# A fused attention, expert and feed-forward kernel: float64 weights converted by one scaling and three bitwise instructions, in pieces twice as wide, with fewer of them in the last expert

## The chip, the cores and the metric

The kernel runs on one core of a Trainium2 chip. The metric is device time in microseconds (us) of one execution; the time before is 629.21, the median of three runs (628.65 to 629.40). The engines are named as in the profile: PE (matmuls; PEld its weight loads), DVE (VectorE), ACT (ScalarE), POOL (GpSimd) and SP (SyncE, which issues most transfers).

## What is computed

Three layers in a row on 1536 tokens of 512 columns: an attention with four sink keys and a window of 128, a mixture of eight experts that gives each token to one of them, and a feed-forward layer with 2048 hidden columns. The change touches the last:

```python
def _moe2_ref(x, w_in, w_out):
    h = x @ w_in
    r = np.maximum(h, 0.0)
    g = r * r
    return (g @ w_out).astype(np.float32)
```

w_in (512 x 2048) and w_out (2048 x 512) arrive as float64, since a float32 array divided or multiplied by a NumPy float64 scalar became float64. Each is 8 MB; the kernel reads them as pairs of 32-bit words and makes float32 values from them.

## The kernel before

**The order of the work.** The kernel is written by hand in the order in which each engine is to run it (a manual schedule), and every engine takes its instructions in that order. First comes the attention, then the eight experts, then the feed-forward layer. Matmuls are done in three products of high and low parts (`h` and `l`): a float32 matrix is rounded to a high part by a copy on ACT, and DVE subtracts that from the value to get the low part.

**Weights come through six buffers.** `raw_tile` gives one of NRAW = 6 buffers of 128 x 1024 words, half a megabyte each. A list `stream` holds all loads in their order: expert weights, then pieces of w_in and w_out. `pull` issues the next loads on SP while buffers are free; `freed` gives one back and, once `eager` is set, pulls at once. A transfer waits on SP until the last reader of its buffer is done, and whatever is behind it on SP waits too.

**A piece.** `piece_load` (L153) fetches one piece of a float64 matrix: for `("i", f)` the 128 hidden columns f of w_in, for `("o", f)` 128 rows of w_out; either is 128 x 512 float64. In the buffer the two words of a value lie side by side, `lo` and `hi`, so each is read and written with a stride of two words. `piece_stage` (L165) converts it in four stages:

- stage 0, on DVE: `lo` is shifted right by 29 and xored with a constant (L173); `hi`, shifted left by 3, is xored into it (L174), which gives the value's magnitude bits; and adding and subtracting 768 leaves the sign in `hi` (L175).
- stage 1, on ACT: the absolute value (L177) and the sign (L178).
- stage 2, on DVE: their product (L180).
- stage 3: the high part by a copy on ACT (L184) and the low part by a subtraction on DVE (L185), after which the buffer is free.

**Ticks.** `Ticks.tick` (L194) moves the conversion on by one: stage 3 of the piece three ticks back (LAG = 3), stage 0 of the next piece, stages 1 and 2 of the one before. The order of the pieces is i0, i1, i2, o0, o1, i3, o2, i4, o3 and so on (L928 to L932). Six ticks lie in the last expert's body, the others in the feed-forward layer, two in each step.

**An expert's body.** `body` (L835) handles one block of 128 tokens: first product in two halves (`g1`), ReLU on ACT (`relu`), transposes of the hidden values with their high and low parts (`tr`, which gives hTh on ACT at L868 and hTl on DVE at L869), second product (`g2`), and a scaling of the result by the gate (`ys`, L911, DVE), which POOL scatters. `plan` is a tuple of six numbers: how many items of `splits` are done in each of the six gaps between these parts. For experts 0 to 6 the items split the next expert's weights; for the last one they are ticks, by the tuple LAST, one in each gap. The body of the last expert also reads the first 512 tokens of the feed-forward layer back (`load_y`, transposes at L964, high and low part x2Ah and x2Al at L969 and L970), at points that the tuple ITS sets.

**The feed-forward layer.** It takes the tokens in four chunks of 512, 512, 256 and 256. A chunk has 16 steps, one per 128 hidden columns. In step f, `stage_a` makes the hidden columns with 12 matmuls (L1045), applies ReLU on ACT (L1047) and squares on DVE (L1048); `stage_g` makes the square's high part gh on ACT (L1056) and low part gl on DVE (L1057); `stage_b` multiplies the columns of the step before with w_out in 12 matmuls (L1069), of which the third is the first to read gl. PE thus takes a(f), b(f-1), a(f+1), b(f) and so on. In the first chunk one tick stands between `stage_a` and `stage_g`, another ahead of `stage_b`. Steps 7, 9, 11 and 13 also transpose 128 tokens each of the next chunk (x2T, x2Bh, x2Bl).

## Time and profile before

| what | value |
|---|---|
| median of three runs | 629.21 us (628.65 to 629.40) |
| the profiled execution | 631.66 us, its span 629.9 us |
| mean granted clock of PE in it | 0.99 of full speed |
| PE busy | 590.4 us, 94% of the span |
| PEld busy | 469.0 us, 74% |
| DVE busy | 377.4 us, 60% |
| ACT busy | 328.3 us, 52% |
| POOL busy | 135.8 us, 22% |
| last expert's body, first block | from about 288 us |
| feed-forward layer | 333.2 us to the end |

Times within the profile are us from the span's start. In rows of instructions in order of time, a number in brackets behind an instruction is how long its engine was idle before it, and behind the arrow what ended that. An engine that is idle costs nothing unless something on the way to the end waits for it.

### The profile page before, as it was taken

To read this page: it belongs to the slowest core of one execution; us is meant where nothing else is said; L and a number is where in the kernel's file an instruction comes from. 1 tells how busy PE (TensorE), PEld (TensorE's weight loads), DVE (VectorE), ACT (ScalarE), POOL (GpSimd) and SP (SyncE) were. 2 spreads that over 40 slices of the span, in tenths; PEclk is the share of its full clock that TensorE was granted. 3 is DMA by queue.
4 is the path that set the end of the run, shared out by engine and by line. 5 is a ranking of instruction groups with operands and counts; after the bars stand their busy time and mean duration, and the time that the engine had idled before them with its cause. 6 is when DMAs were issued, how large, how long until landed. Compare 5 with 4: busy or idle time off the path is not lost. (4 is left out here: it accounts for less than half of the span.)

```text
span 629.9 us, 9961 instructions
## 1 busy us (share of the span) xinstructions
PE 590.4 (94%) x3439; PEld 469.0 (74%) x3439; DVE 377.4 (60%) x943; ACT 328.3 (52%) x745; POOL 135.8 (22%) x235
## 2 busy tenths in 40 slices
PE   8999999969999999998898889889999999999994
PEld 4787777738887777776686667668888888999983
DVE  3788888646349967859826999995323223233321
ACT  4888887526248847656525767763222223233221
POOL 8444643351233323421101000000200001101001
PEclk9999999989999999999999999999999999999998
DMA  8696985345438956957654554530100000100000
GB/s 183 157 227 149 250 164 155 116 138 181 132 102 278 336 194 211 324 157 236 207 195 134 167 167 152 161 107 0 68 1 18 18 0 25 43 0 21 14 2 20
DMA packets 74795, 82.01 MB, mean 130 GB/s; under 512 B 42377, under 2 KB 53641, under 8 KB 74737
## 3 DMA queue, kind: packets, MB, share of 16 engines
q1 hardware_dynamic: 70736, 72.45, 40.1%
q0 software_dynamic: 4000, 8.82, 4.1%
q8 instruction: 32, 0.52, 0.3%
q14 instruction: 27, 0.21, 0.1%
HBM read 69.29 MB, written 16.27 MB: 136 GB/s over the span
## 5 line engine op out<-in xcount | busy, mean ns | idle before, releaser
L1048 DVE TENSOR_TENSOR xb<-xb 128x512 f32<-128x512 f32 (+1 forms) x64 | 35.7, 557 | 109.4 <-ACT xb L1047 109.4
L1047 ACT ACTIVATE xb<-a 128x512 f32<-128x512 f32 (+1 forms) x64 | 31.2, 488 | 116.5 <-PE a L1045 116.5
L1069 PE MATMUL out<-yh,gl 128*128 128x512 f32 x192 | 77.3, 403 | 10.7 <-DVE gl L1057 10.7
L1069 PE MATMUL out<-yh,gh 128*128 128x512 f32 x192 | 76.7, 399 | 0.1
L1069 PE MATMUL out<-yl,gh 128*128 128x512 f32 x192 | 75.9, 395 | 0.0
L1045 PE MATMUL a<-x2Ah,xh 128*128 128x256 f32 (+1 forms) x192 | 61.4, 320 | 0.3 <-PEq L1014 0.3
L1045 PE MATMUL a<-x2Al,xh 128*128 128x256 f32 (+1 forms) x192 | 61.3, 319 | 0.2 <-DVEq L1014 0.2
L1045 PE MATMUL a<-x2Ah,xl 128*128 128x256 f32 (+1 forms) x192 | 61.1, 318 | 0.0
L1077 POOL DMA_INDIRECT out_dram<-oo,tok x12 | 12.0, 998 | 221.9 <-DVE oo L1076 175.5
L447 ACT ACTIVATE p<-p,nm 128x260 f32<-128x260 f32 (+2 forms) x96 | 46.8, 489 | 17.1 <-DVE nm L435 15.9
L1069 PEld LDWEIGHTS out<-yh,gl 128*128 128x128 f32 x192 | 36.1, 188 | 24.7 <-DVE gl L1057 16.6
L1057 DVE TENSOR_TENSOR gl<-xb,gh 128x512 fp32r<-128x512 f32 (+1 forms) x64 | 35.7, 557 | 26.9 <-PE out L1069 14.4
L912 POOL DMA_INDIRECT yd<-ys,dst x14 | 25.3, 1809 | 120.7 <-POOLq L922 50.7
L1056 ACT CAST gh<-xb 128x512 fp32r<-128x512 f32 (+1 forms) x64 | 32.9, 514 | 34.0 <-DVE xb L1048 34.0
L140 DVE TENSOR_TENSOR yl<-raw,yh 128x512 fp32r<-128x512 f32 x64 | 40.4, 685 | 7.8 <-ACT yh L139 6.3
L1069 PEld LDWEIGHTS out<-yh,gh 128*128 128x128 f32 x192 | 36.1, 188 | 7.3 <-ACT gh L1056 1.0
L1069 PEld LDWEIGHTS out<-yl,gh 128*128 128x128 f32 x192 | 36.1, 188 | 7.1
L1045 PEld LDWEIGHTS a<-x2Ah,xh 128*128 128x128 f32 x192 | 36.1, 188 | 5.0 <-issue 0.7
L1045 PEld LDWEIGHTS a<-x2Al,xh 128*128 128x128 f32 x192 | 36.1, 188 | 4.7 <-DVEq L1014 0.5
L1045 PEld LDWEIGHTS a<-x2Ah,xl 128*128 128x128 f32 x192 | 36.4, 189 | 2.9
L139 ACT CAST xh<-raw 128x512 fp32r<-128x512 f32 x64 | 36.3, 619 | 1.0 <-DMA raw<-in_moe_w_dram 0.7
L869 DVE TENSOR_TENSOR hTl<-hT,hTh 128x512 fp32r<-128x512 f32 x28 | 19.3, 690 | 28.9 <-ACT hTh L868 25.7
(201 smaller groups left out, 1466.7 us busy)
## 6 DMA issues: line engine op xcount, KB each, us to landing
raw<-in_moe_w_dram SPq DMA_DIRECT2D x64, 512.0 KB, 5.0
raw<-in_moe_w_in_dram SPq DMA_DIRECT2D x16, 512.0 KB, 4.6
raw<-in_moe_w_out_dram SPq DMA_DIRECT2D x16, 512.0 KB, 3.4
yd<-zero SPq DMA_DIRECT2D x12, 256.5 KB, 5.7
xd<-x SPq DMA_DIRECT2D x12, 256.5 KB, 5.9
xb<-yd SPq DMA_DIRECT2D x12, 256.5 KB, 2.6
kr<-in_k_dram SPq DMA_DIRECT2D x12, 256.0 KB, 4.8
qr<-in_q_dram SPq DMA_DIRECT2D x12, 256.0 KB, 6.3
```

Of the source, the lines that this page charges most:

```text
L139: (hi or nc.scalar.copy)(self.h[i][:, sl], t[:, sl])
L140: (eng or nc.vector).tensor_sub(self.l[i][:, sl], t[:, sl], self.h[i].bitcast(F32)[:, sl])
L447: nc.scalar.activation(d["p"][:, h, :width], d["p"][:, h, :width], AF.Exp, bias=d["nm"][:, h : h + 1], scale=-1.0, accum_out=d["sm"][:, h ...
L869: nc.vector.tensor_sub(l_, p_, h_.bitcast(F32))
L912: nc.gpsimd.indirect_dma_start(out=yd[:, :], out_offset=bass.IndirectOffsetOnAxis(ap=dst[:, b, e : e + 1], axis=0), in_=y_, in_offset=None ...
L1045: nc.tensor.matmul(a_[:, :w], a, bb[:, kk, :w], start=(kk == 0 and m == 0), stop=(kk == KD - 1 and m == 2))
L1047: nc.scalar.activation(r_, a_[:, :w], AF.Relu)
L1048: nc.vector.tensor_mul(r_, r_, r_)
L1056: nc.scalar.copy(gh, r_)
L1057: nc.vector.tensor_sub(gl, r_, gh.bitcast(F32))
L1069: nc.tensor.matmul(outp[c][t], a[:, cs], bb[:, r], start=(f == 0 and m == 0), stop=(f == NFF - 1 and m == 2))
L1077: i = nc.gpsimd.indirect_dma_start(out=out, out_offset=bass.IndirectOffsetOnAxis(ap=tok[:, n : n + 1], axis=0), in_=o_, in_offset=None, bo ...
```

## The change

A piece is now 1024 columns of the destination: two neighbouring old pieces, a megabyte, in one double buffer. Three tiles of 128 x 2048 words take the place of the six buffers; expert weights use their halves as before, and so do the output tiles. A piece of w_in comes by two transfers, one of w_out by one.

The conversion has new instructions. ACT scales `hi`, read as a float32, by 2^-112, which moves the float64 exponent to the float32 one (L181 of the new kernel). DVE shifts `lo` right by 29 (L182), ors `hi` shifted left by 3 into it (L184), and ors the sign bit of `hi` into it (L185). Then follow the high part on ACT (L187) and the low part on DVE (L189). LAG is 1: a tick finishes the piece before and converts the next one up to its last bitwise instruction. There are 17 ticks rather than 35: three in the last expert's body, in its first, fourth and last gap, and one per step of the first chunk, between `stage_a` and `stage_g`; the one ahead of `stage_b` is gone.

```diff
-LAST = (1, 1, 1, 1, 1, 1)
+LAST = (1, 0, 0, 1, 0, 1)
...
+    RAW = [stage.tile([P, 2048], F32, name=f"raw{i}") for i in range(NRAW // 2)]
+
+    def raw_tile(n=1):
+
+        nonlocal slot
+        slot += slot % n
+        t = RAW[slot // 2 % len(RAW)][:, slot % 2 * 1024 : slot % 2 * 1024 + n * 1024]
+        slot += n
+        return t
...
-        while n and stream and held < NRAW:
-            held += 1
+        while n and stream and held + stream[0][0] <= NRAW:
+            held += stream[0][0]
             n -= 1
-            stream.pop(0)()
-
-    def freed():
+            stream.pop(0)[1]()
+
+    def freed(n=1):
...
+        t = raw_tile(2).bitcast(I32)
         if kind == "i":
+            w = 2 * P
+            for x in range(2):
+                nc.sync.dma_start(
+                    t[:, x * 1024 : x * 1024 + 1024].rearrange("p (k n) -> p k n", k=KD),
+                    w_in.rearrange("(k p) f -> p k f", p=P)[:, :, (2 * f + x) * w : (2 * f + x + 1) * w],
+                )
+        else:
             nc.sync.dma_start(
-                t.rearrange("p (k n) -> p k n", k=KD), w_in.rearrange("(k p) f -> p k f", p=P)[:, :, f * P * m : (f + 1) * P * m]
+                t.rearrange("p (t n) -> p t n", t=2), w_out[2 * f * P : 2 * (f + 1) * P, :].rearrange("(t p) n -> p t n", p=P)
             )
...
+        if n == 0:
+            nc.scalar.activation(hi.bitcast(F32), hi.bitcast(F32), AF.Copy, scale=2.0**-112)
+            nc.vector.tensor_scalar(lo, lo, 29, None, op0=ALU.logical_shift_right)
+        elif n == 1:
+            nc.vector.scalar_tensor_tensor(lo, in0=hi, scalar=3, in1=lo, op0=ALU.logical_shift_left, op1=ALU.bitwise_or)
+            nc.vector.scalar_tensor_tensor(lo, in0=hi, scalar=-(2**31), in1=lo, op0=ALU.bitwise_and, op1=ALU.bitwise_or)
+        elif n == 2:
+            nc.scalar.copy(w.h[f], lo.bitcast(F32))
         else:
-            val = t
-        if wide and n == 0:
-            nc.vector.tensor_scalar(lo, lo, 29, 0x40000000, op0=ALU.logical_shift_right, op1=ALU.bitwise_xor)
-            nc.vector.scalar_tensor_tensor(lo, in0=hi, scalar=3, in1=lo, op0=ALU.logical_shift_left, op1=ALU.bitwise_xor)
-            nc.vector.tensor_scalar(sg, sg, 768.0, -768.0, op0=ALU.add, op1=ALU.add)
-        elif wide and n == 1:
-            nc.scalar.activation(val, val, AF.Abs)
-            nc.scalar.activation(sg, sg, AF.Sign)
-        elif wide and n == 2:
-            nc.vector.tensor_mul(val, val, sg)
-        elif n == 3:
-            kind, f = p_
-            w, sl = WI if kind == "i" else WO, slice(f % 2 * 512, f % 2 * 512 + 512)
-            nc.scalar.copy(w.h[f // 2][:, sl], val)
-            nc.vector.tensor_sub(w.l[f // 2][:, sl], val, w.h[f // 2].bitcast(F32)[:, sl])
-            freed()
-
-    LAG = 3
+            nc.vector.tensor_sub(w.l[f], lo.bitcast(F32), w.h[f].bitcast(F32))
+            freed(2)
+
+    LAG = 1
...
-            for d, ns in ((LAG, (3,)), (0, (0,)), (1, (1, 2))):
+            for d, ns in ((LAG, (2,)), (0, (0,)), (LAG, (3,)), (0, (1,))):
...
-    NPRE = 3
-    order = [("i", f) for f in range(NPRE)] + [("o", 0), ("o", 1)]
-    for f in range(NPRE, NFF):
-        order += [("i", f), ("o", f - NPRE + 2)]
-    order += [("o", f) for f in range(NFF - NPRE + 2, NFF)]
+    NPRE = 2
+    order = [("i", f) for f in range(NPRE)]
+    for f in range(NPRE, NFF // 2):
+        order += [("o", f - NPRE), ("i", f)]
+    order += [("o", f) for f in range(NFF // 2 - NPRE, NFF // 2)]
...
-                o_ = stage.tile([P, DM], F32, tag="raw", name="oo", bufs=NRAW)
+                o_ = raw_tile()[:, :DM]
...
-        tick()
         if i >= 1:
             stage_b(*steps[i - 1])
```

On DVE, one step of the first chunk, before: from the square of a step (xb is its hidden columns) up to the first instruction of its second tick. raw is a buffer, x the weights w_in and y those of w_out, h and l their parts.

```order
L1048 TENSOR_TENSOR xb_196<-xb_196 128x512
L185 TENSOR_TENSOR xl_4994<-raw,xh_4993 128x512
L173 TENSOR_SCALAR raw<-raw 128x512
L174 SCALAR_TENSOR_TENSOR raw<-raw 128x512
L175 TENSOR_SCALAR raw<-raw 128x512
L180 TENSOR_TENSOR raw<-raw 128x512
L1057 TENSOR_TENSOR gl<-xb_196,gh 128x512
L185 TENSOR_TENSOR yl_5384<-raw,yh_5383 128x512
```

After the last row the five instructions of a piece follow once more, and then the next square. The same place after the change, with the next square:

```order
L1052 TENSOR_TENSOR xb_199<-xb_199 128x512
L182 TENSOR_SCALAR raw_75<-raw_75 128x1024
L189 TENSOR_TENSOR yl_5290<-raw_74,yh_5289 128x1024
L184 SCALAR_TENSOR_TENSOR raw_75<-raw_75 128x1024
L185 SCALAR_TENSOR_TENSOR raw_75<-raw_75 128x1024
L1061 TENSOR_TENSOR gl<-xb_199,gh 128x512
```

The whole conversion of a step stands between the square and gl; behind gl there is none.

On DVE, the first block of the last expert, before: from the first tick to the evictions of the first tokens.

```order
L173 TENSOR_SCALAR raw<-raw 128x512
L174 SCALAR_TENSOR_TENSOR raw<-raw 128x512
L175 TENSOR_SCALAR raw<-raw 128x512
...
L180 TENSOR_TENSOR raw<-raw 128x512
L869 TENSOR_TENSOR hTl<-hT,hTh 128x512
...
L970 TENSOR_TENSOR x2Al<-x2T,x2Ah 128x4x128
L185 TENSOR_TENSOR xl_4990<-raw,xh_4989 128x512
...
L970 TENSOR_TENSOR x2Al<-x2T,x2Ah 128x4x128 x3
```

And after the change, from the first tick to the gate's scaling:

```order
L182 TENSOR_SCALAR raw_76<-raw_76 128x1024
L184 SCALAR_TENSOR_TENSOR raw_76<-raw_76 128x1024
L185 SCALAR_TENSOR_TENSOR raw_76<-raw_76 128x1024
L873 TENSOR_TENSOR hTl<-hT,hTh 128x512
L182 TENSOR_SCALAR raw_74<-raw_74 128x1024
L189 TENSOR_TENSOR xl_4922<-raw_76,xh_4921 128x1024
...
L974 TENSOR_TENSOR x2Al<-x2T,x2Ah 128x4x128 x4
L182 TENSOR_SCALAR raw_75<-raw_75 128x1024
...
L915 TENSOR_SCALAR ys<-y,gate_2460 128x512
```

One tick, not two, stands ahead of the first hTl, and none between the evictions x2Al; the third stands behind them, ahead of ys.

## Rows read from the trace of the kernel before

**Rows 1.** Busy us by stretch: length, PE, PEld, DVE, ACT, POOL, clock, DMA share, GB/s.

```profile
333.20:436.70 103.50, 92.46 (x387) 70.30 (x388) 93.86 (x171) 69.92 (x119) 2.66 (x5) 1.00 0.43 135
436.70:527.70 91.00, 91.00 (x396) 73.32 (x395) 24.97 (x37) 21.56 (x36) 4.25 (x6) 1.00 0.05 18
```

**Rows 2.** Instructions in order of time: DVE, first half of a step (start, duration).

```profile
357.43 0.68 DVE L1048 TENSOR_TENSOR xb<-xb 128x512 f32<-128x512 f32 x1
358.03 0.68 DVE L185 TENSOR_TENSOR xl<-raw,xh 128x512 fp32r<-128x512 f32 x1
358.63 0.42 DVE L173 TENSOR_SCALAR raw<-raw 128x512 int32<-128x512 int32 x1
359.08 0.69 DVE L174 SCALAR_TENSOR_TENSOR raw<-raw 128x512 int32<-128x512 int32 x1
359.81 0.43 DVE L175 TENSOR_SCALAR raw<-raw 128x512 f32<-128x512 f32 x1
360.15 0.69 DVE L180 TENSOR_TENSOR raw<-raw 128x512 f32<-128x512 f32 x1
360.76 0.68 DVE L1057 TENSOR_TENSOR gl<-xb,gh 128x512 fp32r<-128x512 f32 x1
...
364.09 0.69 DVE L1048 TENSOR_TENSOR xb<-xb 128x512 f32<-128x512 f32 x1
```

**Rows 3.** Instructions in order of time: PE in the same step.

```profile
360.32 0.40 PE L1069 MATMUL out<-yl,gh 128*128 128x512 f32 x1
361.50 0.50 PE L1069 MATMUL out<-yh,gl 128*128 128x512 f32 x1 [0.78 <-DVE gl L1057]
...
363.93 0.39 PE L1045 MATMUL a<-x2Ah,xh 128*128 128x512 f32 x1
...
366.72 0.40 PE L1069 MATMUL out<-yh,gh 128*128 128x512 f32 x1
```

**Rows 4.** Groups by line and shape, whole span: busy us, mean ns | idle before.

```profile
L1048 DVE TENSOR_TENSOR xb<-xb 128x512 f32<-128x512 f32 x32 | 22.1, 689 | 62.1 <-ACT xb L1047 62.1
L1048 DVE TENSOR_TENSOR xb<-xb 128x256 f32<-128x256 f32 x32 | 13.6, 425 | 47.3 <-ACT xb L1047 47.3
L1047 ACT ACTIVATE xb<-a 128x512 f32<-128x512 f32 x32 | 18.9, 591 | 68.0 <-PE a L1045 68.0
L1047 ACT ACTIVATE xb<-a 128x256 f32<-128x256 f32 x32 | 12.3, 385 | 48.5 <-PE a L1045 48.5
L177 ACT ACTIVATE raw<-raw 128x512 f32<-128x512 f32 x32 | 22.5, 702 | 21.9 <-DVE raw L174 17.6 <-ACT yh L184 4.2
```

**Rows 5.** Instructions in order of time: the first step's first matmul, ReLU and square.

```profile
333.24 0.47 PE L1045 MATMUL a<-x2Ah,xh 128*128 128x512 f32 x1 [0.30 <-PEq L1014]
...
336.78 0.60 ACT L1047 ACTIVATE xb<-a 128x512 f32<-128x512 f32 x1 [7.37 <-PE a L1045]
...
337.41 0.69 DVE L1048 TENSOR_TENSOR xb<-xb 128x512 f32<-128x512 f32 x1 [3.62 <-ACT xb L1047]
```

**Rows 6.** Transfers of the page: size each, median us from issue to landing.

```profile
raw<-in_moe_w_in_dram SPq DMA_DIRECT2D x16, 512.0 KB, 4.6
raw<-in_moe_w_out_dram SPq DMA_DIRECT2D x16, 512.0 KB, 3.4
```

**Rows 7.** Instructions in order of time: first tick of the last expert, PE's waits.

```profile
293.07 0.43 DVE L173 TENSOR_SCALAR raw<-raw 128x512 int32<-128x512 int32 x1
...
296.03 0.50 PE L880 MATMUL y<-yh,hTh 128*128 128x512 f32 x1 [0.88 <-ACT hTh L868]
297.48 0.50 PE L880 MATMUL y<-yh,hTl 128*128 128x512 f32 x1 [0.71 <-DVE hTl L869]
301.06 0.14 PEld L964 LDWEIGHTS x2T<-ident,xb 128*128 128x128 f32 x1 [0.38 <-DMA xb<-yd]
302.94 0.50 PE L880 MATMUL y<-yh,hTl 128*128 128x512 f32 x1 [0.75 <-DVE hTl L869]
307.73 0.65 PE L964 MATMUL x2T<-ident,xb 128*128 128x128 f32 x4 [1.28 <-DVE x2Al L970]
```

More of the change, by code (lines that the diff above doesn't have):

```diff
@@ L96 @@
     NRAW = 6
-    stream, held, eager = [], 0, False
-    def raw_tile(dt=F32):
-        return stage.tile([P, 1024], dt, tag="raw", name="raw", bufs=NRAW)
+    stream, held, eager, slot = [], 0, False, 0
+    RAW = [stage.tile([P, 2048], F32, name=f"raw{i}") for i in range(NRAW // 2)]
[5 more added lines that the diff above has]
+        return t
     def pull(n):
         nonlocal held
-        while n and stream and held < NRAW:
-            held += 1
+        while n and stream and held + stream[0][0] <= NRAW:
+            held += stream[0][0]
             n -= 1
-            stream.pop(0)()
-    def freed():
+            stream.pop(0)[1]()
+    def freed(n=1):
         nonlocal held
-        held -= 1
+        held -= n
         if eager:
@@ L142, in split @@
                 freed()
-    wide = w_in.dtype != F32
-    if wide:
-        w_in, w_out = w_in.bitcast(I32), w_out.bitcast(I32)
+    assert mybir.dt.size(w_in.dtype) == 8
+    w_in, w_out = w_in.bitcast(I32), w_out.bitcast(I32)
     WI, WO = Weights(E, wx, "x"), Weights(E + 1, None, "y")
@@ L154, in piece_load @@
         kind, f = p_
-        t = raw_tile(I32) if wide else raw_tile()[:, :512]
-        m = 2 if wide else 1
+        t = raw_tile(2).bitcast(I32)
         if kind == "i":
+            w = 2 * P
[5 more added lines that the diff above has]
+        else:
             nc.sync.dma_start(
-                t.rearrange("p (k n) -> p k n", k=KD), w_in.rearrange("(k p) f -> p k f", p=P)[:, :, f * P * m : (f + 1) * P * m]
+                t.rearrange("p (t n) -> p t n", t=2), w_out[2 * f * P : 2 * (f + 1) * P, :].rearrange("(t p) n -> p t n", p=P)
             )
-        else:
-            nc.sync.dma_start(t, w_out[f * P : (f + 1) * P, :])
         praw[p_] = t
@@ L166, in piece_stage @@
         t = praw[p_]
-        if wide:
-            lo, hi = t.rearrange("p (n t) -> p t n", t=2)[:, 0, :], t.rearrange("p (n t) -> p t n", t=2)[:, 1, :]
-            sg, val = hi.bitcast(F32), lo.bitcast(F32)
-        else:
-            val = t
-        if wide and n == 0:
-            nc.vector.tensor_scalar(lo, lo, 29, 0x40000000, op0=ALU.logical_shift_right, op1=ALU.bitwise_xor)
-            nc.vector.scalar_tensor_tensor(lo, in0=hi, scalar=3, in1=lo, op0=ALU.logical_shift_left, op1=ALU.bitwise_xor)
-            nc.vector.tensor_scalar(sg, sg, 768.0, -768.0, op0=ALU.add, op1=ALU.add)
-        elif wide and n == 1:
-            nc.scalar.activation(val, val, AF.Abs)
-            nc.scalar.activation(sg, sg, AF.Sign)
-        elif wide and n == 2:
-            nc.vector.tensor_mul(val, val, sg)
-        elif n == 3:
-            kind, f = p_
-            w, sl = WI if kind == "i" else WO, slice(f % 2 * 512, f % 2 * 512 + 512)
-            nc.scalar.copy(w.h[f // 2][:, sl], val)
-            nc.vector.tensor_sub(w.l[f // 2][:, sl], val, w.h[f // 2].bitcast(F32)[:, sl])
-            freed()
-    LAG = 3
+        lo, hi = t.rearrange("p (n t) -> p t n", t=2)[:, 0, :], t.rearrange("p (n t) -> p t n", t=2)[:, 1, :]
+        kind, f = p_
+        w = WI if kind == "i" else WO
+        if n == 0:
[6 more added lines that the diff above has]
+            nc.scalar.copy(w.h[f], lo.bitcast(F32))
+        else:
+            nc.vector.tensor_sub(w.l[f], lo.bitcast(F32), w.h[f].bitcast(F32))
+            freed(2)
+    LAG = 1
     class Ticks:
@@ L216, in queue @@
         for i in range(len(w.src)):
-            stream.append(lambda i=i: w.fetch(i))
+            stream.append((1, lambda i=i: w.fetch(i)))
     queue(W[0])
@@ L935 @@
         queue(W[g])
-    stream += [lambda p_=p_: piece_load(p_) for p_ in order]
+    stream += [(2, lambda p_=p_: piece_load(p_)) for p_ in order]
     eager = True
```

## The prediction

> **What bounds the kernel now.** I read the profile from the coarse to the fine. First the busy time by stretch: the second feed-forward layer works through its 1536 tokens in chunks, and the first two chunks issue the same matmuls. The first takes 103.5 us, the second 91.0 [rows 1]. In the second PE is busy all the time. In the first PE has 92.46 of 103.50 and DVE 93.86, and there alone DVE and ACT also convert the float64 weights. So some 11 to 12 us lie in the first chunk as PE waiting, and the question is for whom.
>
> The instructions in order of time answer it. One step of the first chunk runs from one square (L1048, 357.43) to the next (364.09), 6.66 us [rows 2]; it holds two pieces of 512 columns, each with L185, L173, L174, L175, L180, and one L1057; the rows show the first piece. DVE has no gap in it: each instruction starts 0.08 to 0.09 us before its predecessor's end (360.76 after a start at 360.15 of 0.69), or right after it where it reads the predecessor's result (L174 after L173). PE meanwhile stops once a step, before the first matmul that reads gl, the output of L1057: 0.78 us at 361.50 [rows 3]. Twelve matmuls take 2.79 there (363.93 to 366.72), so PE needs 5.6 us per step of 24 and DVE sets 6.66.
>
> **DVE per step afterwards.** A step now converts one piece of 1024 columns. Removed are the two L175, the two L180, and the Abs and Sign on ACT; added per piece a second bitwise instruction with two inputs on DVE and a scaling on ACT. No row has 1024 columns, so I extend: L1048 takes 689 ns for 512 and 425 for 256, thus 264 per 256 columns and 161 fixed [rows 4]; 1024 columns take 0.69 + 0.53 = 1.22. I use that for the low-part subtraction and both two-input bitwise instructions (L174 today: 0.69). The shift today takes 0.42 with 512 columns, so its columns cost half as much, and 1024 take 0.42 + 0.26 = 0.69; that one operation fewer keeps this rate is my choice. From the start of the square to the end of gl, with 0.085 of overlap at each free hand-over and 0.035 of gap between the two bitwise ones: square 0.605, shift 0.605, subtraction 1.135, first bitwise 1.26, second 1.14, gl 0.69, together **5.44**. From square to square it is 5.35 if nothing else delays it, against 6.66 now and 5.6 for PE.
>
> **The loop behind it.** DVE under PE's 5.6 doesn't yet make PE the bound, because gl now stands at the end of the whole tick. After gl(f) come ten matmuls of the second product (2.34, plus 0.06 to start), twelve of the first product of step f+2 (2.80), then the last one's remainder, ReLU on ACT and the hand-overs, then square to gl again. Without its late start the first step would give 3.64 from first matmul to square: the rows show 4.17 (333.24 to 337.41), of which 0.53 is the delay of the early matmuls, since ReLU starts at 336.78, 3.54 after the first, where 3.01 is the regular lag [rows 5]. So the loop is 2.40 + 3.64 + 5.44 = 11.48 for two steps, 5.74 per step: just over PE, with DVE waiting a little in every second step.
>
> **First chunk, summed.** The first gl ends 4.17 + 5.44 = 9.6 us after the first matmul. Six loops lead to gl(12): 68.9. Then PE runs alone to the second chunk: 2.34 and four times 2.80, 13.5. Four x2T evictions lie in this stretch on DVE at 0.60 each; I count 0.6 for what isn't hidden. Sum 92.6 against 103.5: **10.9 saved**. That PE alone sets the rest would give 92.2 (31 groups of 2.80, 1.7 for transposes, and 3.6 until the first gl), so little more is there. The other end: if shift, subtraction and bitwise instructions pay their fixed part twice (twice today's rows: 0.84, 1.37, 1.38), the loop grows by 0.6 to 12.1, 0.3 a step; thirteen steps and the first gl then give back 4.5. I take the linear extension, since two sizes of the same instruction show it.
>
> ACT has per step ReLU and gh, about 0.6 each, cast and scaling. From 591 for 512 columns and 385 for 256, the latter two take 0.70 + 0.41 = 1.11 at most [rows 4]: 3.4 of 5.7, no bound. The cast is there 1.1 after ReLU, the scaling 2.1; DVE asks for them 1.2 and 2.4 after. That is close but covered. If that cover is gone by 0.2, the loop grows by 0.2, some 1.3 in all.
>
> **Loads.** Three slots of a megabyte replace six of half. A slot is free after the subtraction, 2.4 after its step's square, and wanted by the shift two steps on: 11.48 - 2.43 + 0.6 = 9.6 us later. Half a megabyte lands in 4.6 (w_in) and 3.4 (w_out) [rows 6]; even twice that, 9.2 and 6.8, fits, and the two halves of w_in go out back to back. Cost nothing. SP issues them in the order of the ticks, behind the same reads of yd as before; POOL's queue is the same. The output tiles take halves of the same slots long after; nothing.
>
> **The last expert.** Its first block had six ticks, now three, but the same three megabytes are begun, so the chunk starts the same 13 of 16. PE's waits there: 0.88 for hTh, 0.71 and 0.75 for hTl, 1.28 for x2Al [rows 7]. DVE begins the first tick at 293.07 either way. Shift and two bitwise ones take 3.0, so hTl starts at 296.1 and its matmul at 296.8, not 297.48. The next tick takes 4.14, so the second hTl is done at 301.5, before PE asks: PE still waits for the tokens until 301.06 and reaches that matmul at 302.0, not at 302.94 (the wait of 0.75, and 0.17 by which matmuls otherwise overlap). The third tick now stands behind all four x2A evictions, so the 1.28 goes: 0.92 + 1.28 = 2.2. The last transposes, 307.73 today, come at 305.5; with them (0.65) and their evictions (0.6 each) the third tick starts at 307.4, takes 4.14, and ys (about 0.7) behind it ends at 312.2. The next block's first hTl is then done at 312.9; PE asks for it 26 matmuls and four transposes, 6.6, after 305.9, at 312.5: 0.4 is given back. Two things can take more: on ACT the first scaling stands ahead of the first half's ReLU and waits for its load, and the load that the first subtraction frees is now a whole megabyte among the reads of the tokens. **1.8 saved**; the bounds are 0, where these eat it all, and 3.6, the sum of the four waits.
>
> **Sum.** 10.9 + 1.8 = 12.7. The profiled execution took 631.66 (span 629.9), so 619.0 (617.2); the median of the runs, 629.21, lies 2.45 lower, and from it I forecast **616.5**.
>
> **Rivals.**
> 1. *DVE stays the bound*, because the shift loses its rate (1.22, not 0.69) or the longer ones don't extend linearly. For: no row has this form. Against: L173 and L175 both run at 0.42 to 0.43 with other operations. 0.53 per step raises the loop to 12.0 and DVE to 5.9; with gaps 4 us are lost: 620.5. Chance 0.15.
> 2. *Each DVE instruction starts only when the last has finished.* Then five overlaps of 0.085 per step vanish, DVE goes to 5.8 and the loop to 11.9, about 3 us: 619.5. The rows speak against it: 0.61 from start to start at a duration of 0.69 [rows 2]. Chance 0.02. The Trainium skill (VectorE: DVE Perf Modes, The DRAIN you can't avoid) says that the next operation doesn't start until the pipe is empty; it would give this time, and by its duration the trace disagrees, as far as a row's end is the pipe's end.
> 3. *Slower: the loads become the wait.* With a landing time L, two steps take L + 1.9. Today's step with the expert's gain is matched at 6.8, so L = 11.7 decides; at 13 a step is 7.45, twelve steps lose 1.7 each, 20.5, and the run takes 637. For it: a slot frees only as a whole, and one load covers what two did. Against: 3.4 and 4.6 for half the size. Chance 0.03, and 0.03 for loads that cost a few us but not all.
> 4. *It does only half:* the waits just move in the expert, or ACT's cast or scaling comes late in the chunk, as hTl and gl stand behind longer blocks. 619 to 622. Chance 0.07.
>
> **How the numbers follow.** The forecast has 0.70, with 614.5 to 619. The range reaches down to 614, where all 3.6 of the expert's waits go and the chunk is PE's alone (629.21 - 11.3 - 3.6 = 614.3), and up to 621.5, which takes in most of rivals 1, 2 and 4. A difference of 0.2%, 1.3 us, can be told from none. Faster than that is all but rival 3 and mishaps: 0.95; within it 0.02, since a cost would have to meet the gain; slower 0.03.
>
> **What would show it.** In the changed profile: the first chunk takes 92 to 94 with PE near 95% or more; squares stand 5.6 to 5.9 apart; two-input instructions of 1024 take 1.22, the shift 0.69, the scaling 1.1; waits for gl fall from 0.8 a step to 0.1 or so, the first apart; the last expert's first block loses the 1.28. Wrong would be: a shift over 1 us, squares over 6.2 apart, the shift waiting for a load, or hTl's waits in the expert as long as before.

## The result, and the profile after

The changed kernel takes 622.99 us (median of 5 runs, 622.56 to 625.19) against 629.21 in the same comparison: ratio 0.9901, 95% interval 0.9877 to 0.9925. It is faster by 6.2 us, half of the 12.7 I had summed, and lies outside my range (614 to 621.5).

The busy time by stretch, as in [rows 1] for the kernel before (length, PE, PEld, DVE, ACT, POOL, clock, DMA share, GB/s):

```profile
333.20:427.70 94.50, 91.47 (x388) 71.77 (x389) 77.86 (x90) 48.15 (x63) 3.39 (x5) 0.98 0.44 142
427.70:518.70 91.00, 91.00 (x397) 73.35 (x396) 24.89 (x37) 21.56 (x36) 4.25 (x6) 1.00 0.05 18
```

The first chunk falls from 103.5 to 94.5: 9.0 saved. DVE's share goes from 93.86 of 103.50 to 77.86 of 94.50, and its instructions last what I had worked out; here is the first step, DVE in order of time (start, duration), which answers to [rows 2]:

```profile
337.32 0.69 DVE L1052 TENSOR_TENSOR xb<-xb 128x512 f32<-128x512 f32 x1 [3.62 <-ACT xb L1051]
337.93 0.69 DVE L182 TENSOR_SCALAR raw<-raw 128x1024 int32<-128x1024 int32 x1
338.53 1.22 DVE L189 TENSOR_TENSOR yl<-raw,yh 128x1024 fp32r<-128x1024 f32 x1
339.67 1.22 DVE L184 SCALAR_TENSOR_TENSOR raw<-raw 128x1024 int32<-128x1024 int32 x1
340.92 1.23 DVE L185 SCALAR_TENSOR_TENSOR raw<-raw 128x1024 int32<-128x1024 int32 x1
342.06 0.69 DVE L1061 TENSOR_TENSOR gl<-xb,gh 128x512 fp32r<-128x512 f32 x1
```

PE's instructions around that gl show what I had not foreseen:

```profile
340.30 0.39 PE L1073 MATMUL out<-yl,gh 128*128 128x512 f32 x1
342.80 0.55 PE L1073 MATMUL out<-yh,gl 128*128 128x512 f32 x1 [2.11 <-DVE gl L1061]
343.15 0.63 PE L1073 MATMUL out<-yh,gh 128*128 128x512 f32 x1
343.58 0.63 PE L1073 MATMUL out<-yl,gh 128*128 128x512 f32 x1
...
346.55 0.40 PE L1073 MATMUL out<-yh,gl 128*128 128x512 f32 x1
346.79 0.39 PE L1049 MATMUL a<-x2Ah,xh 128*128 128x512 f32 x1
```

The wait was expected. Behind it matmuls follow each other at 0.43 us where they take 0.23 elsewhere, and the ten of this product need 4.0 us (342.80 to 346.79) instead of the 2.34 that I counted. The granted clock, the first of the last three numbers, says why:

```profile
342.00:344.00 2.00, 1.20 (x3) 0.95 (x4) 2.00 (x5) 1.82 (x2) 0.79 (x2) 0.78 0.94 311
344.00:346.00 2.00, 2.00 (x6) 1.60 (x5) 2.00 (x2) 0.92 (x2) 0.00 (x0) 0.50 0.39 135
```

At 0.50 PE runs at 1.2 GHz, its lower level. Before that it had been idle for 0.49 us (up to 339.96) and, two matmuls later, for 2.11 us.

In the last expert nothing was won. DVE's first tick starts at 290.18 there, 2.89 before that of [rows 7], but the feed-forward's first matmul stands at 333.15 against 333.24. First SP's instruction in order of time (the first of the token reads), then PE's waits from 275 to 350 by line (us in total, times, longest):

```profile
298.48 1.29 SPq L962 DMA_DIRECT2D xb<-yd  x3
```

```profile
PE x2T L968 <- DMA xb<-yd: 3.6, 1, 3.6
PE out L1073 <- DVE gl L1061: 2.1, 1, 2.1
PE y L884 <- DVE hTl L873: 1.5, 1, 1.5
PE out L1073 <- ACT gh L1060: 0.5, 1, 0.5
```

The waits for hTh and x2Al of [rows 7] and the second one for hTl are gone, but the first for hTl has grown from 0.71 to 1.5, as much as both were before. PE now also stands 3.55 us for the first token tile, and here too matmuls run 0.43 apart afterwards, up to 305.3, at a granted clock of 0.54 and 0.61 in the two stretches of 2 us from 302.

The end of the expert now hangs on the fourth and last token tile. In the changed kernel its read stands on SP behind the megabyte that the second tick freed (two halves, L165), and it lands 5.1 us after its issue, as POOL's copy from the tile shows; PE's last transposes start behind that:

```profile
299.86 0.93 SPq L165 DMA_DIRECT2D raw<-in_moe_w_in_dram  x2
301.89 0.34 SPq L962 DMA_DIRECT2D xb<-yd  x1
307.01 0.18 POOL L970 COPY tok<-xb 128x1 int32<-128x1 int32 x1 [3.69 <-DMA xb<-yd]
307.10 0.63 PE L968 MATMUL x2T<-ident,xb 128*128 128x128 f32 x4
```

Before, half a megabyte stood ahead of that read, it landed 3.5 us after its issue, and the last transposes (307.73 in [rows 7]) waited for x2Al:

```profile
300.18 0.33 SPq L162 DMA_DIRECT2D raw<-in_moe_w_out_dram  x1
301.80 0.32 SPq L958 DMA_DIRECT2D xb<-yd  x1
305.28 0.18 POOL L966 COPY tok<-xb 128x1 int32<-128x1 int32 x1 [2.56 <-DMA xb<-yd]
```

### The profile page after: what moved, and what is told of

It is laid out like the page before. It is cut to its first block, busy times and chain, and to the rows that moved or that the text cites. A ratio compares the mean times of both kernels' runs of the same rounds, so it can differ in the third digit from the quotient of the medians.

```text
span 620.8 us, 9781 instructions
## 1 busy us (share of the span) xinstructions
PE 588.8 (95%) x3437; PEld 470.4 (76%) x3439; DVE 359.6 (58%) x847; ACT 305.1 (49%) x681; POOL 136.3 (22%) x235
## 5 line engine op out<-in xcount | busy, mean ns | idle before, releaser
L1081 POOL DMA_INDIRECT out_dram<-raw,tok x12 | 12.0, 998 | 215.4 <-DVE raw L1080 168.9
L916 POOL DMA_INDIRECT yd<-ys,dst x14 | 25.5, 1819 | 116.2 <-POOLq L926 50.5
L145 ACT CAST yh<-raw 128x512 fp32r<-128x512 f32 x64 | 35.5, 624 | 2.6 <-PEq L926 1.7
```

The source lines that it names most:

```text
L145: (hi or nc.scalar.copy)(self.h[i][:, sl], t[:, sl])
L916: nc.gpsimd.indirect_dma_start(out=yd[:, :], out_offset=bass.IndirectOffsetOnAxis(ap=dst[:, b, e : e + 1], axis=0), in_=y_, in_offset=None ...
L1081: i = nc.gpsimd.indirect_dma_start(out=out, out_offset=bass.IndirectOffsetOnAxis(ap=tok[:, n : n + 1], axis=0), in_=o_, in_offset=None, bo ...
```

## The experiments

So that executions with a different start can be compared, I measure lengths inside each profile: from the ys of the last but one expert (the start of that DVE instruction, called Y) to SP's first token read, the last expert from Y to the first matmul of the feed-forward, and the first chunk from there to the first matmul of the second chunk that the trace shows (103.7 for before and 94.7 for the changed kernel by this count). The scatter is issued 1.52 to 1.54 after Y in all of them, and SP holds the first token read until it has landed; "landing" is the time from the scatter's issue to that read. Each ratio is to the runs of the kernel before in the same comparison (medians 629.2 to 630.8).

| kernel | landing | expert from Y | first chunk | median us | ratio, interval |
|---|---|---|---|---|---|
| before | 7.1 | 43.46 | 103.7 | 629.21 | 1 |
| changed | 10.1 | 46.33 | 94.7 | 622.99 | 0.9901 (0.9877 to 0.9925) |
| before_again | 7.1 | 43.47 | 103.7 | 628.8, one | |
| g_first | 8.8 | 45.83 | 95.7 | 623.56 | 0.9896 (0.9878 to 0.9914) |
| ticks_late | 6.5 | 43.97 | 94.7 | 623.31 | 0.9899 (0.9881 to 0.9918) |
| pe_filled | 8.7 | 45.60 | 93.2 | 620.69 | 0.9860 (0.9840 to 0.9880) |
| tick_ahead | 8.8 | 45.45 | 90.7 | 618.35 | 0.9823 (0.9791 to 0.9856) |
| load_late | 6.1 | 47.43 | 94.8 | 625.17, one | |
| quarters | 8.9 | 45.37 | 96.0 | 625.35, one | |
| late_ahead | 8.8 | 46.33 | 90.6 | 619.65 | 0.9837 (0.9814 to 0.9860) |
| act_load | 6.3 | 42.79 | 90.6 | 618.07 | 0.9791 (0.9763 to 0.9818) |
| act_load_late | 6.2 | 44.33 | 90.6 | 617.78 | 0.9795 (0.9766 to 0.9824) |
| bits_only | 8.0 | 42.76 | 92.2 | 617.95 | 0.9797 (0.9771 to 0.9823) |
| bits_ahead | 7.6 | 42.29 | 93.0 | 619.25 | 0.9822 (0.9799 to 0.9845) |

The two lengths explain the times. Against before_again the changed kernel has +2.9 and -9.0, together -6.1, and the medians differ by 6.2. The expert's length in turn follows the start of PE's last token transposes, which is 17.95 after Y in both executions of before and 20.28 in the changed kernel: from there to the first matmul of the feed-forward it is 26.0 to 26.1 in every kernel with pieces of 1024 (load_late 26.9) and some 25.5 in those with pieces of 512.

### before_again

No edit.

> The kernel before, a second profiled execution. Theory (the profiled execution of before lay 2.4 us above its median because PE waited 2.4 us once near 133 us for a token read of the first experts, ahead of everything the change touches): that wait is absent here, the last expert's first tick lies near 290.5 instead of 293.07, the first feed-forward matmul near 331, and the execution takes about 629 us; the change then loses some 2 us in the last expert and gains 9 in the first chunk. Rival (the 2.45 us are spread over the kernel, or the wait is always there): first feed-forward matmul again within 0.5 us of 333.2, and the gain of the change is then 9 us less something after the first chunk.

The theory held in what matters: the first matmul comes 2.82 earlier than in [rows 5], and Y 2.83 earlier, so the difference lies ahead of Y. The wait that the theory names, PE's for the first experts' tokens (it ends at 137.67 in the first execution and at 136.40 here), is not absent but 1.0 instead of 2.4, and accounts for half of it.

```profile
330.42 0.47 PE L1045 MATMUL a<-x2Ah,xh 128*128 128x512 f32 x1 [0.30 <-PEq L1014]
```

The lengths that I argued from are the same in both executions (43.46 and 43.47), so the slow start of the profiled run did not mislead the sum. It hid the loss at first sight: the changed kernel's expert is 2.9 us longer, not equal.

### g_first

```diff
             stage_a(c, f)
+            if i == 0:
+                stage_g(c, f)
             tick()
-            stage_g(c, f)
+            if i > 0:
+                stage_g(c, f)
```

> The changed kernel with one edit: in the feed-forward's first step alone the split of g (gh and gl) is issued ahead of the tick, so gl no longer stands behind 4.4 us of bitwise work. Theory A (the missing 1.9 us of the first chunk are a stall of 0.49 + 2.11 us for gh and gl, and ten matmuls at a granted clock of about .50 behind it): the wait for gl goes, what is left is at most 1.5 us for the split of the weights of the second product, the granted clock stays at 1.00 between 342 and 348, the first chunk falls from 94.5 to 90.5-92, and the time from 623.0 to 619.5-621. Rival B (the first steps are bound by VectorE whatever the order: the wait turns up one step later at the same size): first chunk 94-95, time 622.5-623.5.

Rival B held in kind, and the chunk, 95.7, is a little over its range. PE's waits by line:

```profile
PE out L1073 <- DVE gl L1061: 1.8, 1, 1.8
...
PE out L1073 <- DVE yl L189: 0.9, 1, 0.9
PE out L1073 <- issue: 0.7, 1, 0.7
```

The first gl is early, then PE waits for the weights' low part and for the second gl. The tick's 4.4 us must be done somewhere before PE's second or third product, and reordering behind the first square doesn't make room. The granted clock stays at 1.00 up to 350, behind the first two waits, but the third one, which ends at 350.18, is followed by the lower level once more:

```profile
350.00:352.00 2.00, 1.82 (x6) 1.43 (x7) 2.00 (x4) 2.00 (x3) 0.00 (x0) 0.72 0.64 254
352.00:354.00 2.00, 2.00 (x6) 1.57 (x5) 1.97 (x3) 0.30 (x1) 0.00 (x0) 0.50 0.12 29
```

So both costs, the wait and the slow matmuls behind it, only moved one step on.

### ticks_late

`LAST = (1, 0, 0, 1, 0, 1)` becomes `(0, 0, 0, 1, 1, 1)`.

> The changed kernel with its three first ticks in the last expert's fourth, fifth and sixth gap instead of the first, fourth and sixth: VectorE is nearly idle when the scatter of the block before is issued by POOL. Theory D (the scatter, whose rows POOL writes out, is held up while VectorE works without a gap): from issue to landing the scatter takes 3-6 us instead of 10.1, the token reads behind it start by 294-295, PE's wait of 3.55 us for the first token tile falls under 0.5, the clock stays at 1.00 there, and the first feed-forward matmul comes 3-6 us earlier, unless the first chunk gives it back; time 617-620. Rival E (the scatter's landing is set by the transfers of weights or by the scatter itself): landing 9-11 us as before, PE's wait for the token tile 3.5-5 us because the wait of 1.48 us for hTl is gone, time 622-623.5.

The profile had a landing of 6.5 and an expert of 43.97, not far from what theory D wanted, but the time is that of the changed kernel. Late_ahead, with the same last expert, has 8.8 and 46.33 (below): the ticks alone don't explain what this one profile shows.

### pe_filled

```diff
         g2([2, 3])
+        if e == E - 1 and b == 0:
+            pre(e, 1)
+            idle(14)
...
+        if i == 1:
+            idle(11)
         if i >= 1:
             stage_b(*steps[i - 1])
```

`idle(n)` issues n matmuls of zeros into a bank that nobody reads; `pre(e, 1)` is the same as before, ahead of them.

> The changed kernel with products of zeros put where PE only waits: 14 ahead of the first token tile's transposes in the last expert (14 x 0.2335 = 3.3 us of the 3.55 us wait) and 11 ahead of the first product with the second weights (2.6 us of the 0.49 + 2.11 us). Nothing that is waited for comes earlier. Theory A (a clock lowered after PE stood idle is a cost of its own): the granted clock stays at 1.00 at 302-306 and 342-347, the six matmuls and eight transposes behind the first wait and the ten matmuls behind the second take their 0.2335 us each again, which gives back some 1.9 and 1.8 us; time 619-620. Rival F (the slow stretches come from something else, transfers or the operands): they stay at 0.43 us per matmul and the time at 622.5-623.5.

Theory A, for the chunk (the time of 620.69 is 0.7 above what it gave): 93.2, which is 1.6 less, with the work that is waited for no earlier. The clock in the stretches shown above:

```profile
342.00:344.00 2.00, 1.51 (x7) 0.92 (x6) 2.00 (x4) 1.49 (x2) 0.96 (x2) 1.00 0.92 291
344.00:346.00 2.00, 2.00 (x10) 1.63 (x9) 2.00 (x3) 1.23 (x2) 0.00 (x0) 1.00 0.66 228
```

Ten matmuls instead of six in 344 to 346, at a clock of 1.00. In the expert the gain doesn't show: 45.60, where other executions of the same order without zeros have 45.83 and 45.45. PE's clock stayed at 1.00 there, but it then stood before the fourth token tile, which landed 19.5 after Y, no earlier than in the other two (19.7 and 19.3):

```profile
307.45 0.63 PE L976 MATMUL x2T<-ident,xb 128*128 128x128 f32 x4 [1.65 <-DMA xb<-yd]
```

### tick_ahead

```diff
+            if i == 0:
+                tick()
             stage_a(c, f)
-            tick()
+            if i > 0:
+                tick()
             stage_g(c, f)
```

> The changed kernel with one edit: in the feed-forward's first step the tick is issued ahead of the first a, not behind its square, so that VectorE does the 4.4 us of bitwise work in the 3.6 us in which it waits for the first a (333.7 to 337.3 in the changed kernel). Theory A2 (the missing 2 us of the first chunk, 94.7 against 92.6, come from 4.4 us of VectorE work that stands in front of gl while VectorE had just been idle, and from the lowered clock that follows the 2.11 us stall): no wait over 1 us for gh, gl or the weights in the first three steps, granted clock 1.00 from 338 to 350, first chunk 92.0-93.0, time 620.5-621.5. Rival B2 (the first steps are bound by VectorE's sum of work, as g_first's 95.65 allows; the wait only moves to the second or third step and the clock falls there): first chunk 94-96, time 622.5-624.

Theory A2, and more than it asked: the chunk takes 90.7, 4.1 less, about the 2.6 of both waits and the 1.6 of the clock. The time falls to 618.35, below the expected range, with an interval that doesn't touch the changed kernel's. DVE in order of time:

```profile
334.06 0.70 DVE L182 TENSOR_SCALAR raw<-raw 128x1024 int32<-128x1024 int32 x1 [0.23 <-DVEq L1018]
...
337.06 1.23 DVE L185 SCALAR_TENSOR_TENSOR raw<-raw 128x1024 int32<-128x1024 int32 x1
338.20 0.69 DVE L1052 TENSOR_TENSOR xb<-xb 128x512 f32<-128x512 f32 x1
339.62 0.69 DVE L1061 TENSOR_TENSOR gl<-xb,gh 128x512 fp32r<-128x512 f32 x1 [0.73 <-PE a L1049]
```

The tick now fills the time in which DVE waited for the first square. The wait for the first gl was no property of the new instructions but of the place of the first tick in the feed-forward.

### load_late

The load of the first w_out piece, which SP starts 3.2 after Y, is held back until the token reads are on SP's queue:

```diff
-        while n and stream and held + stream[0][0] <= NRAW:
+        while n and stream and held + stream[0][0] <= NRAW and (len(stream) != wall[0]):
...
+    wall[0] = len(order) - 2
...
             its = load_y(0, ("bg", "bg"))
+            wall[0] = -1
+            pull(NRAW)
```

> The changed kernel with one load moved: the 1 MB piece of the second weights that SP starts 3.2 us after the ys of the last but one expert now stands behind the token reads on SP's queue, so it moves while no scatter is under way. Theory L (the scatter's rows wait for that load's transfers): from issue to landing the scatter takes 5-7 us instead of 8.6-10.1, and the first token read starts 7-8 us after that ys instead of 10.2-11.7. Theory D (the scatter's rows are held by VectorE's work, whatever else moves): landing still 8.6-10.1. Either way the token tiles now share the engines with nothing that is ahead of them; a load that comes late for the third tick would show as a wait of VectorE or ScalarE for it near 312 us.

Theory L: landing 6.1, token read 7.7 after Y. What the queues moved (packets, MB, share; q1 the loads, q0 the scatter) in the changed kernel at 290.8 to 292.8, at 292.8 to 293.8 and at 293.8 to 295.8, so 4 to 6, 6 to 7 and 7 to 9 after Y:

```profile
q1 hardware_dynamic: 83, 0.32, 82.3%
...
q1 hardware_dynamic: 105, 0.43, 106.9%
...
q1 hardware_dynamic: 87, 0.29, 37.2%
q0 software_dynamic: 75, 0.18, 23.7%
```

And in load_late at 290.8 to 292.8 and 292.8 to 293.8, which is 2.5 to 4.5 and 4.5 to 5.5 after Y:

```profile
q1 hardware_dynamic: 404, 0.40, 59.0%
...
q0 software_dynamic: 74, 0.18, 48.4%
```

In both the scatter's 80 packets move only when the loads ahead of them are nearly through; in the changed kernel that is a megabyte more. The kernel as a whole is no better, since the fourth token read now stands behind the loads in its turn, and PE waits 4.83 us for that tile.

### quarters

The shift and the bitwise instructions of the first two pieces are cut into four of 256 columns each.

```diff
+    def parts(p_, lo, hi):
+        if p_ in (("i", 0), ("i", 1)):
+            return [(lo[:, x : x + 256], hi[:, x : x + 256]) for x in range(0, 1024, 256)]
+        return [(lo, hi)]
...
-            nc.vector.tensor_scalar(lo, lo, 29, None, op0=ALU.logical_shift_right)
+            for a, b in parts(p_, lo, hi):
+                nc.vector.tensor_scalar(a, a, 29, None, op0=ALU.logical_shift_right)
```

> The changed kernel with the shift and the two bitwise instructions of the first two pieces cut into four instructions of 256 columns each; the same work, some 0.5 us longer in each tick. Theory D1 (each long VectorE instruction holds POOL's descriptor writing until it ends; shorter ones leave more gaps, as the shorter instructions of the kernel before did with a landing of 7.0 us): the scatter lands in 6-8 us. Theory D2 (what counts is that VectorE has no idle time, however it is cut): landing 8.6-11 us. Theory L (transfers alone): 8.6-10.1 us as well.

Landing 8.9: not D1. D2 fell with late_ahead. In the chunk, at 96.0, PE waits as in the changed kernel (2.2 us for gl, 0.5 for gh), and the granted clock is 0.50 from 344 to 350, longer than there.

### late_ahead

The edits of ticks_late and tick_ahead together.

> Both edits together: the three ticks in the last expert's fourth, fifth and sixth gap, and the feed-forward's first tick ahead of the first a. If the two losses are separate (theory A2 for the chunk; the ticks in the scatter's time for the expert), the expert ends about 44.0 us after the ys of the one before it instead of 45.6-46.3 and the first chunk takes 92.0-93.0: time 618-620. If the first chunk is bound by VectorE's sum (B2) it takes 94-96: time 621-624.

The chunk as in tick_ahead; the expert at 46.33 with a landing of 8.8, though DVE had no tick in the scatter's time. PE waits 3.9 us for the first token tile, and the granted clock is 0.50 from 300 to 306, where it was 1.00 in ticks_late; PE's waits for the tokens and x2Al are no longer in sum (4.1 against 4.5), so it is the low clock that makes the same order 2.4 us longer here. Theory D falls as far as the ticks go: in act_load (below) they lie in the scatter's time, and it lands in 6.3. The Trainium skill (SBUF — State Buffer, "🔬 SBUF: two separate sides", the box on the "DVE blocks DMA" trap) says that a VectorE instruction in a mode that takes both ports keeps GpSimd from writing the descriptors of its DMAs. That was where D came from. Whether the instructions here run in such a mode no row shows; the landing, with ticks or without, did not follow VectorE's work. The Trainium skill (DMA: Bandwidth & Descriptors, "🔬 Queues, rings and completion order") also has each DMA engine take turns between the queues, packet by packet. In ticks_late both queues did move together; in the changed kernel no packet of q0 is seen while 188 of q1 pass (4 to 7 after Y); whether its rows were in the queue by then no row shows.

### act_load

On tick_ahead: the same load, held back from SP as in load_late, is issued by ACT behind the first hTh, 4.0 us after Y (291.90).

```diff
-            nc.sync.dma_start(
+            (nc.scalar if f == 0 else nc.sync).dma_start(
                 t.rearrange("p (t n) -> p t n", t=2), w_out[2 * f * P : 2 * (f + 1) * P, :].rearrange("(t p) n -> p t n", p=P)
...
         tr(0)
+        if e == E - 1 and b == 0:
+            wall[0] = -1
+            pull(1)
```

> The kernel tick_ahead with one more edit: the 1 MB load of the first piece of the second weights is issued by ACT behind the last expert's first hTh, some 5 us after the ys of the expert before, not by SP at 3.2. Theory L (the scatter's rows move only when the loads that were queued ahead of them are through; the queue's packets stood at 7 to 9 us in four executions, behind this load, at 4 to 5 us in load_late, where it was not there, and at 3 to 4 us in ticks_late, where they came in just ahead of it): packets of the scatter at 3.5-6 us, landing 5-7 us after issue instead of 8.8, the first token read at 6.5-8.5 us instead of 10.3, PE's wait for the first token tile under 1 us instead of 2.2, no wait of 4.8 us for the fourth tile as in load_late; the expert ends 43-44.5 us after that ys instead of 45.45, and the time falls from 618.35 to 616-617.5. Rival M (the scatter lands late for another reason, or the load, now between scatter and token reads, holds the tokens instead): PE's waits for token tiles stay at 2-4 us in sum and the time at 618-620.

In the profile, theory L: landing 6.3, PE's waits for token tiles 1.2 us in sum,

```profile
PE x2T L974 <- DMA xb<-yd: 1.2, 2, 1.1
```

and the expert at 42.79, 2.7 shorter than tick_ahead's. The time, 618.07 (runs from 615.96 to 618.81), lies above L's range and just in M's; its interval overlaps tick_ahead's, so by time the two are not told apart. The profiled execution, 615.96, was the fastest of the five. The expert's length and the token waits in it are what speaks for L.

### act_load_late

Act_load with the ticks of ticks_late.

> The kernel act_load with the three ticks in the fourth, fifth and sixth gap of the last expert. Theory L as in act_load, and in addition no wait of 1.5 us for the first hTl, but a wait for x2Al of up to 2.5 us before the fourth token tile, as in ticks_late, since VectorE has as much to do and only the order differs: the expert ends 42.5-44 us after that ys, time 615.5-617.5. Rival M: token tiles hold PE for 3.5-4 us as in late_ahead (46.3 us), time 619-620.

44.33, a little over what was expected, as is the time. PE waits 2.4 us for the first token tile and 2.5 for x2Al. The landing is short (6.2), so L holds, but the order with ticks late is the worse one, since PE gets to the tokens sooner and x2Al stands behind a tick.

### bits_only

The kernel before, with the arithmetic of the change alone; pieces, loads and ticks as before.

```diff
-            nc.vector.tensor_scalar(lo, lo, 29, 0x40000000, op0=ALU.logical_shift_right, op1=ALU.bitwise_xor)
-            nc.vector.scalar_tensor_tensor(lo, in0=hi, scalar=3, in1=lo, op0=ALU.logical_shift_left, op1=ALU.bitwise_xor)
-            nc.vector.tensor_scalar(sg, sg, 768.0, -768.0, op0=ALU.add, op1=ALU.add)
+            nc.scalar.activation(sg, sg, AF.Copy, scale=2.0**-112)
+            nc.vector.tensor_scalar(lo, lo, 29, None, op0=ALU.logical_shift_right)
         elif wide and n == 1:
-            nc.scalar.activation(val, val, AF.Abs)
-            nc.scalar.activation(sg, sg, AF.Sign)
+            nc.vector.scalar_tensor_tensor(lo, in0=hi, scalar=3, in1=lo, op0=ALU.logical_shift_left, op1=ALU.bitwise_or)
+            nc.vector.scalar_tensor_tensor(lo, in0=hi, scalar=-(2**31), in1=lo, op0=ALU.bitwise_and, op1=ALU.bitwise_or)
         elif wide and n == 2:
-            nc.vector.tensor_mul(val, val, sg)
+            pass
```

> The kernel before with one part of the change alone: scaling on ACT, shift and two bitwise instructions in place of the two bitwise instructions, the rounding, the multiply, Abs and Sign; pieces of 512 columns, two ticks a step, six ticks in the last expert and loads of 512 KB stay. Theory S (what the change gains in the first chunk comes from the operations on VectorE, and wider pieces add little): a piece takes VectorE 2.3 us from start to start instead of 2.73, a step 5.8 instead of 6.66 against PE's 5.6, the first chunk 92-95.5; the scatter lands in 7 us as before, the expert ends at 43.5 us after the ys ahead of it; time 619-621.5. Rival W (half of the gain comes from the width of the pieces, by the fixed part of each instruction, 161 ns): first chunk 96.5-99, time 623-625.5.

Theory S, and faster than it said: 617.95, ratio 0.9797, against 0.9901 for the whole change; the intervals don't touch. The landing, 8.0, was not the 7 of before, and PE waited 2.5 us for the first token tile; the expert is still the shorter one, 42.76. DVE in order of time, half a step, to be held against [rows 2]:

```profile
352.05 0.69 DVE L1047 TENSOR_TENSOR xb<-xb 128x512 f32<-128x512 f32 x1
352.65 0.69 DVE L184 TENSOR_TENSOR xl<-raw,xh 128x512 fp32r<-128x512 f32 x1
353.26 0.42 DVE L174 TENSOR_SCALAR raw<-raw 128x512 int32<-128x512 int32 x1
353.59 0.69 DVE L176 SCALAR_TENSOR_TENSOR raw<-raw 128x512 int32<-128x512 int32 x1
354.32 0.70 DVE L177 SCALAR_TENSOR_TENSOR raw<-raw 128x512 int32<-128x512 int32 x1
354.93 0.69 DVE L1056 TENSOR_TENSOR gl<-xb,gh 128x512 fp32r<-128x512 f32 x1
...
357.80 0.68 DVE L1047 TENSOR_TENSOR xb<-xb 128x512 f32<-128x512 f32 x1
```

A step takes 5.75 (352.05 to 357.80) instead of 6.66, and gl comes 2.88 after the square's start, not 4.74 (342.06 from 337.32) as behind a piece of 1024. So the first gl costs PE only 1.0 us, and the granted clock stays at 1.00 there. The wide pieces make DVE's work a little shorter, and gl later.

### bits_ahead

Bits_only with tick_ahead's edit.

> The kernel bits_only with the edit of tick_ahead: the first of the two ticks of the feed-forward's first step is issued ahead of the first a. Theory A2 (VectorE's idle 3.6 us before the first square can hide a tick, and the first wait for gl is what is left of the first chunk's loss): the wait of 1.0 us for the first gl goes, the first chunk falls from 92.16 to 90.6-91.3 and the time by 0.9-1.5 us to 616.5-617.1, near act_load. Rival (with two short ticks a step VectorE's 5.75 us a step keeps gl late by some 0.1 a step whatever the start): first chunk 91.8-92.2, time 617.5-618.5.

A miss by both expectations: 93.0 and 619.25. The wait for gl is gone, but ACT's gh is held up (ACT in order of time):

```profile
336.53 0.60 ACT L1046 ACTIVATE xb<-a 128x512 f32<-128x512 f32 x1 [5.97 <-PE a L1044]
340.26 0.62 ACT L1055 CAST gh<-xb 128x512 fp32r<-128x512 f32 x1 [3.14 <-DMA yd<-ys,dst]
```

PE waits 1.6 us for it, and the granted clock is 0.60 and 0.55 in the two stretches of 2 us from 342. ACT waits for the expert's last scatter. That was issued at 334.29, and the tick freed a buffer so early that SP's next load went out at 334.41; the scatter's rows moved between 337 and 339, behind it (landing 6.0). In tick_ahead the load went out 1.33 after the scatter, whose rows came first (landing 4.2); in the changed kernel no load was near, and it landed in 3.3. The queue's order again, at another place.

## Why the prediction was wrong

**What held.** The cost of the instructions: shift 0.69, two-input instructions 1.22, square to gl 5.44 (337.32 to 342.75 is 5.43), the first gl 9.6 after the first matmul (342.75 - 333.15 = 9.60). Scaling and cast took 1.19 and 1.13 where I had at most 1.11, without consequence. The loop of two steps was to take 11.48 and takes 11.6 (squares at 356.09, 367.72 and 379.35). The loads cost nothing in the chunk. Rival 1 did not happen. Nor did rival 2: the shift starts 0.61 after the square's start at a duration of 0.69.

**The first chunk: 10.9 foreseen, 9.0 measured.** The step that failed is "After gl(f) come ten matmuls of the second product (2.34, plus 0.06 to start)" for the first of them. I had the wait in the sum but not what it does to the clock: those ten took 4.0. Filling the wait gave back 1.6 of the missing 1.9, so this part is shown. I also took the wait itself for unavoidable: the 92.2 that I gave for PE alone contains 3.6 us until the first gl. Tick_ahead's 90.7 lies under that floor.

**The last expert: 1.8 saved foreseen, some 2.4 lost.** Three executions of the changed order (46.33, g_first's 45.83, tick_ahead's 45.45) average 45.9 against 43.47. My bounds were 0 and 3.6 saved; a loss I had excluded. The step that failed is "PE still waits for the tokens until 301.06" with "SP issues them in the order of the ticks, behind the same reads of yd as before; POOL's queue is the same". The token reads wait for the landing of POOL's scatter, and I took that as fixed. So "The last transposes, 307.73 today, come at 305.5", 15.7 after Y, failed too: they started 19.4 to 20.3 after Y in those three executions, when the fourth tile had landed. Two loads of a megabyte stand in the way. The one among the token reads, which the prediction named as able to eat the gain, holds up the fourth read (5.1 to 6.0 us from issue to landing instead of 3.5). The one ahead of the scatter it had not looked at. Without a load there the landing is 6.1 to 6.3 in three executions (load_late, act_load, act_load_late); with the megabyte it is 8.7 to 10.1 in six and 6.5 in one (ticks_late); with half of one, in pieces of 512, 7.1 to 8.0 in four. In act_load, where only this load was moved, the last transposes start 16.7 after Y and the expert is 2.7 shorter than tick_ahead's. That rests on lengths within single executions: the times of the two kernels are not told apart. The first matmul with hTl came 0.4 earlier than before (7.31 after Y against 7.70), not 0.7, which was of no use to PE, as the tokens were then missing. Behind the last transposes another 0.5 went (26.0 instead of 25.5), close to the 0.4 that I gave back.

**The sum.** 1.9 and 4.2 are 6.1 of the 6.5 us between 12.7 and 6.2. The 2.45 us by which the profiled run stood above its median lay ahead of Y and played no part. Of the rivals the fourth came nearest ("the waits just move in the expert"), at 0.07 and with too small a price. What I gave 0.70 rested on the costs of instructions, which were right, and on token reads that stay where they are, which was wrong; transfers had a chance only through the loads' duration (rival 3).

**What stays open.** Whether the scatter's rows are held in the queue or are written late, which the packets' times alone don't tell, and why they slipped in ahead of the load in ticks_late, with the same instructions as late_ahead. POOL's instruction for the scatter gives a hint. It is shorter in ticks_late than in any other execution (the rest have 2.5 to 2.65), here beside late_ahead's:

```profile
290.50 1.32 POOL L916 DMA_INDIRECT yd<-ys,dst  x1 [10.19 <-POOLq L926]
289.58 2.53 POOL L916 DMA_INDIRECT yd<-ys,dst  x1 [10.20 <-POOLq L926]
```

It ends 2.85 after Y there, ahead of the load's issue at 3.18, and at 4.06 in late_ahead, behind it. The same holds at the end of the expert: in tick_ahead it ends at 335.61, ahead of the load at 335.91, and in bits_ahead at 335.27, behind the load at 334.41. That the one which is complete first goes first fits these rows and is no more than that, since spans on POOL are rough; why it was shorter in ticks_late stays open.

## What to carry to other kernels

When a change makes transfers larger or frees a buffer earlier, look for the small transfer that will stand behind them, and follow who waits for its landing: here a 0.19 MB scatter, four reads behind it, PE behind those; and the last of those reads may have a load of its own in front. When work is merged into wider pieces, the sum of an engine may fall while the one result that the next engine waits for comes later; the arithmetic alone, in the old pieces, was worth 12.8 us, all parts together 6.2 (11.5 with one tick moved, tick_ahead). And where an engine idles just before a stall, move work into that idle time before reordering behind it, and see which load this sets free earlier: in bits_ahead that cost the first chunk 0.8 us.

## What was not expected of the hardware

An idle PE cost more than its idle time: after waits of 0.49 and 2.11 us the granted clock was 0.78, 0.50 and 0.87 in the three stretches of 2 us from 342 to 348, and filling the wait gave back 1.6 us. It was not so each time: g_first's wait of 2.18 us for the first token tile left the clock at 1.00, and tick_ahead's of 2.19 was followed by 0.50. Nor did a low clock always cost time: in the changed kernel's expert PE reached the fourth token tile, slowly, just as it had landed.

A scatter of 80 packets landed in 3.3 us with no load near (at the end of the changed kernel's expert), and in 6.0 to 10.1 behind loads.
